# A linear-attention, GLU and MLP kernel: the first MLP pair by whole products, and a rotated decoding of GLU weights

## The chip, the cores and the metric

The kernel runs on one core of one Trainium2 chip. The metric is the device time of one execution in microseconds (us), here the median of 3 runs.

## What is computed

Three stages, all float32 in and out, cut from the reference; the weights come in as float64:

```python
q_p, k_p = phi(q * scale), phi(k * scale)         # 4 batches, 8 heads, 576 tokens, 128 random features
kv = einsum('bhsm,bhsd->bhmd', k_p, v); z = sum(k_p, axis=2)
x = (q_p @ kv) / (q_p @ z + 1e-06)                # heads side by side: 2304 tokens x 512
xn = x / sqrt(mean(x * x) + 1e-06) * rms_g
x = (silu(xn @ w_gate) * (xn @ w_val)) @ w_out    # GLU, 512 -> 1536 -> 512
out = silu(x @ w_in) @ w_out2                     # MLP, 512 -> 2048 -> 512
```

## The kernel before

**Numbers.** Every operand of a product is kept as a high and a low float32 part, and a product is three matmuls (`PASS`, line 191: high x high, high x low, low x high). A high part is made by ScalarE, the low one by VectorE as the difference (for example `split_h`, lines 196 to 200).

**Tiles.** The 2304 tokens are blocks 0 to 3 of 512 and block 4 of 256 columns. The 12 chunks of 128 columns of the GLU's inner side go three in the sweeps at the start (`sweeps`) and nine in groups u0 to u8 of one chunk each; the MLP's 16 chunks are eight pairs u9 to u16. The tiles `xs` hold the input of a stage (high and low), `ya` the sums of its output, `tok` the token sums. PSUM has four banks of tag `g` and four of tag `y`, used in turn; a product takes the next bank of its tag and waits until that has been read.

**One group.** `quad` (line 514) makes the two products of blocks 0 and 1 (gate and value, or the pair's two chunks) as seven half products, in the manner of Winograd, which need sums of the two weights (`sum12`, `sum34`) and of the tokens of blocks 0 and 1 (`tok[1]` to `tok[4]`, line 311 on). `glu_block` (line 601) and `g1_mlp` (line 233) make the other blocks by whole products. Between these pieces come the output products of earlier blocks (`g2_glu`, `g2_mlp`), a chunk at a time; VectorE adds each chunk to `ya` (line 271). In the last GLU group each chunk, once complete, is split into `xs` for the MLP by ScalarE (line 273) and VectorE (line 250).

**Token sums.** `first_sums` (line 340) makes those of the GLU from high plus low, all adds on GpSimd; `token_sums` (line 367) makes those of the MLP from `ya` in place, on GpSimd, during the last GLU group. ScalarE splits off the high half (line 329), VectorE the low one (line 332).

**Weights.** `w_load` (line 130) has SP fetch 512 KB of float64 into `raw0` or `raw1`; `w_decode` (line 141) turns them into float32 by five operations on VectorE (lines 146 to 157) and two integer adds on GpSimd (line 160). ScalarE scales a gate's or a value's weight by rms_g (line 168) and makes the high half (line 434), VectorE the low half (line 438).

**Order.** The program's order on each engine is the order in which Python emits it. `stream` (line 625) yields after each piece with the time that it costs TensorE. The driver (line 1448 on) adds that up and, in between, pops one part of the token sums after more than `T_PACE` = 1.2 us, or one job of `WeightQueue` (line 390) after more than `M_PACE` = 2.0, unless `hold` is set; `need` takes jobs early where a product wants them. The jobs of a group are the list in `plan` (line 467). Each engine works through its own instructions in that order.

Of the kernel before, what the change touches and what calls it, by code (L numbers as in the profile page):

```python
# [20 lines left out]
def kernel(  # L21
# [221 lines left out]
    def g2_glu(fs, j, hs, first, last):  # L243
# [3 lines left out]
        keep = KC // 2 if j == 1 else 0  # L247
# [7 lines left out]
        for d in range(KC):  # L255
# [57 lines left out]
    tok, sums, ready = {}, [], set()  # L313

    def w_tile(side, slot):
        pool = pools["w"][2] if side and slot < W_EARLY else pools["w"][side]
        return pool.tile([P, 2 * KC * P], F32R, tag=f"w{side}_{slot}", name=f"w{side}_{slot}")
# [22 lines left out]
    def first_sums():  # L340
# [3 lines left out]
        def temp(k, pool, tag):  # L344
            tl = pool.tile([P, KH * TB * P], F32, tag=tag, name=tag, **({"bufs": 1} if pool is rawp else {}))
            u[k] = tl.rearrange("p (c t) -> p c t", c=KH)

        def whole(k, j, h, pool, tag):
            temp(k, pool, tag)
            less(u[k], half(j, 0, h), half(j, 1, h), ALU.add)  # L350

        return [
            lambda: whole(1, 1, 0, rawp, "raw0"),
            lambda: whole(0, 0, 0, rawp, "raw1"),
            lambda: less(u[0], u[1], u[0]),
            lambda: whole(2, 1, 1, pools["w"][1], "w1_7"),
# [5 lines left out]
            lambda: whole(3, 0, 1, rawp, "raw0"),  # L362
# [1124 lines left out]
```

## Time and profile before

| | |
|---|---|
| Median of 3 runs | 976.98 us (974.52 to 978.86) |
| Profiled execution | 977.74 us |
| Its span | 975.9 us |
| Busy: TensorE, VectorE, ScalarE, GpSimd | 949.0, 712.4, 437.2, 429.6 us |
| Granted clock, mean over the span | 0.99 |

The profile is of one execution. The span runs from its first to its last instruction; the execution's own time includes what lies around it. Shares of busy time are means over stages with different limits, so the stretches are looked at one by one below. In the rows PE is TensorE (PEld its weight loads), DVE is VectorE, ACT ScalarE, POOL GpSimd, SP SyncE, and SPq its DMA queue. A row of a timeline has the start in us, the time that the x instructions of the row take together, the engine, the line, the operation, output<-input, and in brackets how long the engine was idle ahead of it and what released it. PEclk is TensorE's granted clock as a share of full speed.

### The profile page before, as it was taken

What the parts mean: (1) busy time and instruction counts of PE and PEld (TensorE: products, weight loads), DVE (VectorE), ACT (ScalarE), POOL (GpSimd) and SP (SyncE); (2) the same over time, 40 slices, a digit from 0 to 9 for tenths busy, and PEclk for the clock granted to TensorE, in tenths of its full rate; (3) what the DMA queues carried; (4) which work ended last, traced back from release to release, by engine and by line L of the source; (5) the groups of instructions that cost most, each with busy time, mean ns of one, the idle gap of its engine ahead of it and who ended that gap; (6) DMA issues with size and microseconds to landing.
All of it is one profiled execution on the core that took longest, in us unless ns stands there. A gap on an engine that the chain in (4) does not pass through costs nothing.

```text
span 975.9 us, 17017 instructions
## 1 busy us (share of the span) xinstructions
PE 949.0 (97%) x6558; PEld 793.0 (81%) x6558; DVE 712.4 (73%) x1366; ACT 437.2 (45%) x986; POOL 429.6 (44%) x414
## 2 busy tenths in 40 slices
PE   8999999999999999999999969999999999999998
PEld 6888878888787888888888847888888888888887
DVE  6998989667677698788778887547575767676643
ACT  6999886533323324433332344644243333333321
POOL 8888745625336354435445252424333332424200
PEclk9999999999999999999999979999999999999999
DMA  7655543012101121021112000202021111111023
GB/s 192 166 134 132 142 125 98 1 44 58 51 22 60 49 65 33 33 65 43 44 44 65 22 22 22 65 20 68 22 65 27 60 41 46 44 44 44 1 75 119
DMA packets 79488, 60.40 MB, mean 62 GB/s; under 512 B 27312, under 2 KB 73648, under 8 KB 79408
## 3 DMA queue, kind: packets, MB, share of 16 engines
q1 hardware_dynamic: 79136, 59.26, 21.0%
q8 instruction: 51, 0.84, 0.4%
q14 instruction: 29, 0.24, 0.1%
q10 hardware_dynamic: 272, 0.07, 0.0%
HBM read 49.87 MB, written 4.72 MB: 56 GB/s over the span
## 4 chain that ended last, share of the span: by engine, by line
PE 83%; DVE 9%; ACT 2%; POOL 2%; issue 2%; DMA 1%; SPq 1%; DVEq 0%; POOLq 0%; ACTq 0%
PE y L295 20%; PE g L205 17%; PE g L508 16%; PE y L260 10%; PE y L205 5%; PE b L957 3%; PE b L205 3%; POOL m L160 2%; PE kv L1037 2%; PE b L1357 2%; PE b L930 2%; PE b L1141 2%; DVE ya L271 1%; DVE xs L250 1%; PE b L1237 1%
## 5 line engine op out<-in xcount | busy, mean ns | idle before, releaser
L160 POOL TENSOR_TENSOR m<-m,raw 128x512 int32<-128x512 int32 x136 | 202.6, 1493 | 337.6 <-issue 179.9
L205 PE MATMUL g<-xs,w 128*128 128x512 f32 x960 | 233.1, 390 | 0.0
L205 PEld LDWEIGHTS g<-xs,w 128*128 128x128 f32 x960 | 180.0, 188 | 37.0
L295 PE MATMUL y<-w,h 128*128 128x512 f32 (+1 forms) x870 | 206.9, 388 | 0.0
L295 PEld LDWEIGHTS y<-w,h 128*128 128x128 f32 x870 | 162.5, 188 | 33.6
L260 PE MATMUL y<-h,w 128*128 128x512 f32 (+1 forms) x648 | 159.2, 373 | 12.1 <-ACT s L614 4.9
L199 DVE TENSOR_TENSOR h<-s,h 128x512 fp32r<-128x512 f32 (+1 forms) x134 | 103.0, 773 | 68.0 <-ACT h L198 66.5
L260 PEld LDWEIGHTS y<-h,w 128*128 128x128 f32 x648 | 115.1, 192 | 35.8 <-ACT s L614 5.3
L271 DVE TENSOR_TENSOR ya<-y,ya 128x512 f32<-128x512 f32 (+1 forms) x200 | 122.6, 630 | 23.3 <-PE y L260 22.9
L198 ACT ACTIVATE h<-s 128x512 fp32r<-128x512 f32 (+1 forms) x134 | 77.1, 585 | 114.1 <-DVE s L611 68.6
L306 DVE TENSOR_TENSOR ya<-y,ya 128x512 f32<-128x512 f32 (+1 forms) x127 | 84.3, 679 | 56.9 <-PE y L295 56.3
L508 PE MATMUL g<-xs,w 128*128 128x512 f32 x408 | 105.2, 393 | 0.0
L438 DVE TENSOR_TENSOR w<-m,w 128x512 fp32r<-128x512 f32 x67 | 65.9, 984 | 39.3 <-ACT w L434 39.3
L434 ACT ACTIVATE w<-m 128x512 fp32r<-128x512 f32 x76 | 47.9, 630 | 99.6 <-POOL m L160 89.6
L508 PEld LDWEIGHTS g<-xs,w 128*128 128x128 f32 x408 | 76.8, 190 | 16.0
L508 PE MATMUL g<-w,w 128*128 128x512 f32 x306 | 78.8, 393 | 3.2 <-DVE s L536 2.2
L1006 ACT ACTIVATE e<-b,nb 128x128 f32<-128x128 f32 x272 | 76.1, 425 | 7.2 <-issue 4.0
L508 PEld LDWEIGHTS g<-w,w 128*128 128x128 f32 x306 | 56.7, 188 | 15.9 <-DVE s L536 2.4
L205 PEld LDWEIGHTS y<-xs,w 128*128 128x128 f32 x480 | 61.4, 191 | 6.2 <-DVE ya L271 3.9
L205 PE MATMUL y<-xs,w 128*128 128x256 f32 x480 | 62.5, 283 | 3.1 <-DVE ya L271 3.1
L974 DVE TENSOR_REDUCE small<-b 128x4 f32<-128x512 f32 (+1 forms) x80 | 51.3, 642 | 7.1 <-PE b L957 3.6
L531 ACT ACTIVATE s<-s 128x512 f32<-128x512 f32 x25 | 15.8, 632 | 81.9 <-DVE s L536 81.9
(122 smaller groups left out, 1186.2 us busy)
## 6 DMA issues: line engine op xcount, KB each, us to landing
raw<-in_moe_w_out_dram SPq DMA_DIRECT2D x28, 512.0 KB, 3.6
raw<-in_moe_w_in_dram SPq DMA_DIRECT2D x16, 512.0 KB, 3.7
raw<-in_moe_w_gate_dram SPq DMA_DIRECT2D x12, 512.0 KB, 3.6
raw<-in_moe_w_val_dram SPq DMA_DIRECT2D x12, 512.0 KB, 3.6
qT<-e SPq DMA_DIRECT2D x72, 64.0 KB, 2.5
x<-in_k_dram SPq DMA_DIRECT2D x16, 256.0 KB, 3.8
x<-in_q_dram SPq DMA_DIRECT2D x16, 256.0 KB, 3.3
va<-in_v_dram SPq DMA_DIRECT2D x32, 128.0 KB, 4.1
```

The lines of the kernel that those rows point to most:

```text
L160: tt(out=mi, in0=mi, in1=(low if step == 5 else high).bitcast(I32), op=ALU.add)
L198: nc.scalar.activation(out=ht[:, 0, :], in_=s, func=AF.Copy)
L199: nc.vector.tensor_tensor(out=ht[:, 1, :], in0=s, in1=ht[:, 0, :].bitcast(F32), op=ALU.subtract)
L205: nc.tensor.matmul(out=ps, lhsT=w[:, a, cc * P:(cc + 1) * P], rhs=xs[j][:, c, cc, :], start=(n == 0), stop=(n == 3 * KC - 1),)
L260: nc.tensor.matmul(out=ps, lhsT=wt[1, "o", f][:, a, d * P:(d + 1) * P], rhs=hs[f][:, c, :], start=(n == 0), stop=(n == nn - 1),)
L271: nc.vector.tensor_tensor(out=y[:, d, :], in0=ps, in1=y[:, d, :], op=ALU.add)
L295: nc.tensor.matmul(out=ps, lhsT=hs[f][:, a, t * P:(t + 1) * P], rhs=wt[2, "p", f][:, c, d0:d1], start=(n == 0), stop=(n == nn - 1),)
L306: nc.vector.tensor_tensor(out=o[:, t, d0:d1], in0=ps, in1=o[:, t, d0:d1], op=ALU.add)
L438: eng.tensor_tensor(out=v[:, 1, :], in0=x, in1=v[:, 0, :].bitcast(F32), op=ALU.subtract)
L508: nc.tensor.matmul(out=ps, lhsT=w[:, a, (c0 + c) * P:(c0 + c + 1) * P], rhs=x(b, c), start=(start and n == 0), stop=(n == 3 * KH - 1), ski ...
L974: nc.vector.tensor_reduce(out=st.mx.rearrange("p (j e) -> p e j", e=2)[:, e], in_=st.ps[e], axis=AX.X, op=ALU.max)
L1006: nc.scalar.activation(out=st.e[r][:, :, h, :] if blocks4 else st.e[r][:, h, :], in_=src.rearrange("p (a f) -> p a f", a=4) if blocks4 els ...
```

## The change

1. The first MLP pair (`std`) has no `quad`: blocks 0 and 1 are done by whole products, with the last output chunks of the GLU's blocks 2, 3 and 4 ahead of each.
2. The last GLU group does its output chunks one per piece like the other groups, and splits all of block 1 into high and low like the other blocks.
3. The token sums of the MLP are made during that pair, from high plus low of `xs`, by one function for both stages; its four adds of high and low (`whole`) go to VectorE, the four differences stay on GpSimd.
4. The first value weight (u0) is loaded, and the weight queue released, in the last part of the first token sums.
5. The jobs of a GLU group are rotated: value before gate, and the high and low half of the output weight of the group before stand between the two decodes.

The core of the diff (left out: arguments for types, and the job list of the later MLP pairs, which is the old one with its loads at other jobs):

```diff
         nn = 3 * len(fs)
-        keep = KC // 2 if j == 1 else 0
...
-            if last and d >= keep:
+            if last:
                 nc.scalar.activation(out=xs[j][:, 0, d, :], in_=y[:, d, :], func=AF.Copy)
-                if d > keep:
+                if d:
                     low(d - 1)
-                if d == KC - 1:
-                    low(d)
-            if last and j == 1 and d == KC - 1:
-                sums.extend(token_sums())
             yield nn * blocks[j] / 2365
+        if last:
+            low(KC - 1)
...
+    std = next(u for u, g in enumerate(groups) if g[0] == 2)
...
-    def first_sums():
+    def token_sums(temp, end):
         half = lambda j, a, h: xs[j][:, a, KH * h:KH * (h + 1), :].bitcast(F32)
         u = {}
...
-        def whole(k, j, h, pool, tag):
-            temp(k, pool, tag)
-            less(u[k], half(j, 0, h), half(j, 1, h), ALU.add)
-
...
+        def whole(k, j, h):
+            u[k] = u[1] if k == 3 else temp(k).rearrange("p (c t) -> p c t", c=KH)
+            nc.vector.tensor_tensor(out=u[k], in0=half(j, 0, h), in1=half(j, 1, h), op=ALU.add)
+
+        ready.clear()
         return [
-            lambda: whole(1, 1, 0, rawp, "raw0"),
-            lambda: whole(0, 0, 0, rawp, "raw1"),
+            lambda: whole(1, 1, 0),
+            lambda: whole(0, 0, 0),
             lambda: less(u[0], u[1], u[0]),
-            lambda: whole(2, 1, 1, pools["w"][1], "w1_7"),
+            lambda: whole(2, 1, 1),
             lambda: less(u[1], u[2], u[1]),
             lambda: less(u[2], u[2], u[0]),
             lambda: tok_high(3, u[1]),
             lambda: (tok_low(3, u[1]), tok_high(2, u[2])),
             lambda: tok_low(2, u[2]),
-            lambda: whole(3, 0, 1, rawp, "raw0"),
+            lambda: whole(3, 0, 1),
             lambda: less(u[3], u[3], u[2]),
             lambda: None,
             lambda: tok_high(4, u[3]),
-            lambda: tok_low(4, u[3]),
-            lambda: wq.load(0, 0, 0),
+            lambda: (tok_low(4, u[3]), end(0)),
         ], [
             lambda: tok_high(1, u[0]),
-            lambda: tok_low(1, u[0]),
-            lambda: wq.load(0, 1, 1),
-        ]
-
-    def token_sums():
-        y0, y1 = (ya[j].rearrange("p (c t) -> p c t", c=KC) for j in (0, 1))
-        a0, b0, a1, b1 = y0[:, :KH], y0[:, KH:], y1[:, :KH], y1[:, KH:]
-        ready.clear()
-        return [
-            lambda: less(a1, a1, a0),
-            lambda: less(b1, b1, a1),
-            lambda: (tok_high(1, a1), less(a0, b1, a0)),
-            lambda: (tok_low(1, a1), tok_high(2, b1), less(b0, b0, b1)),
-            lambda: tok_low(2, b1),
-            lambda: tok_high(3, a0),
-            lambda: tok_low(3, a0),
-            lambda: tok_high(4, b0),
-            lambda: tok_low(4, b0),
+            lambda: (tok_low(1, u[0]), end(1)),
...
-            for slots, *fns in [
-                (0, lambda: dec(a0, 0)),
-                (0, lambda: dec(a1, 1), lambda: self.load(u, bs[0], 0)),
-                (1, lambda: hi(a0), lambda: two and self.load(u, bs[1], 1)),
-                (1, lambda: lo(a0), lambda: hi(a1)),
-                (0, lambda: lo(a1), sum12),
-                (0, sum34),
-                (1, lambda: shi(0)),
-                (0, lambda: slo(0)),
-                (1, lambda: shi(1), lambda: dec(bs[0], 0), lambda: two or self.load(u + 1, 1, 1)),
-                (0, lambda: slo(1), lambda: self.load(u + 1, 0, 0)),
-            ]:
-                self.jobs.append((slots, fns))
-            if two:
...
+            load = self.load
+            if kind == 1:
+                jobs = [
+                    (0, lambda: dec(a1, 1), lambda: load(u + 1, 1, 1)),
+                    *self.tail,
+                    (0, lambda: dec(a0, 0), lambda: load(u, bs[0], 0)),
+                    (1, lambda: hi(a1)),
+                    (0, lambda: lo(a1)),
+                    (1, lambda: hi(a0)),
+                    (0, lambda: lo(a0), sum12),
+                    (0, sum34),
+                    (1, lambda: shi(0)),
+                    (0, lambda: slo(0), lambda: dec(bs[0], 0), lambda: load(u + 1, 0, 0)),
+                    (1, lambda: shi(1)),
+                    (0, lambda: slo(1)),
+                ]
+                self.tail = [(1, lambda: hi(bs[0])), (0, lambda: lo(bs[0]))]
+            elif u == std:
+                jobs = [
+                    *self.tail,
+                    (0, lambda: dec(a1, 1), lambda: load(u, bs[1], 1)),
+                    (0, lambda: dec(a0, 0), lambda: load(u, bs[0], 0)),
+                    (0,),
+                    (1, lambda: hi(a1)),
+                    (1, lambda: lo(a1), lambda: hi(a0)),
+                    (0, lambda: lo(a0), lambda: dec(bs[0], 0), lambda: load(u + 1, 0, 0)),
+                    (0, lambda: dec(bs[1], 1), lambda: load(u + 1, 1, 1)),
+                    (0,),
+                    (1, lambda: hi(bs[0])),
+                    (1, lambda: lo(bs[0]), lambda: hi(bs[1])),
+                    (0, lambda: lo(bs[1])),
                 ]
             else:
...
+        def end(n):
+            wq.load(0, n, n)
+            wq.hold = n == 0
...
             if n == 2:
                 sums.extend(later)
-                wq.hold = False
                 wq.free += [(0, k) for k in range(6)]
...
-            done = kind == 1 and groups[u + 1][0] == 2
+            done = u + 1 == std
             hs = {j: {} for j in range(NB)}
-            yield from quad(u, iter(pend), hs)
-            if u:
+            if u == std:
+                out_of = lambda j: g2_mlp(fs, j, hs[j], True, False, False)
+                ys = iter(pend)
+                now, later = token_sums(
+                    lambda k: w_tile(1, 7, F32) if k == 2 else wq.slot(("t", k), F32),
+                    lambda n: wq.release(("t", 1 - n)),
+                )
+                yield from g1_mlp(fs[0], 0, hs[0], (), take(ys, 4))
+                yield from g1_mlp(fs[1], 0, hs[0], (), take(ys, 4))
+                sums.extend(now)
+                yield from g1_mlp(fs[0], 1, hs[1], (), ys)
+                wq.release(*wq.keys(u - 1)[1])
+                yield from g1_mlp(fs[1], 1, hs[1], (), out_of(0))
+                sums.extend(later)
+                yield from g1_mlp(fs[0], 2, hs[2], (), out_of(1))
+                yield from g1_mlp(fs[1], 2, hs[2], (), ())
+            else:
+                yield from quad(u, iter(pend), hs)
...
                 ys = chain_of(out_of(0), out_of(1))
-                k = 2 if done else 1
-                yield from glu_block(f, 2, hs[2], ys, {"g": 0, "v": k})
-                yield from glu_block(f, 3, hs[3], ys, {"g": k, "v": 2 - k})
+                yield from glu_block(f, 2, hs[2], ys, {"g": 0, "v": 1})
+                yield from glu_block(f, 3, hs[3], ys, {"g": 1, "v": 1})
                 yield from glu_block(f, 4, hs[4], ys, {"g": 1, "v": 1})
                 yield from ys
                 pend = chain_of(out_of(2), out_of(3), out_of(4))
-                if done:
-                    yield from out_of(2)
-                    pend = chain_of(out_of(3), out_of(4))
...
         for c in stream():
             due += c
-            if sums:
-                if due > T_PACE:
-                    sums.pop(0)()
+            if sums and due > T_PACE:
+                sums.pop(0)()
+                if wq.hold:
                     due = 0.0
-            elif due > M_PACE and not wq.hold and wq.tick():
+            if due > M_PACE and not wq.hold and (wq.tick() or sums):
                 due = min(due - M_PACE, M_PACE)
 
 
```

**How it moves instructions.** Two places, both on VectorE, with what each instruction waits for in brackets (DMAHW is a transfer). Lines 199, 228, 146 to 157 are the same in both kernels; line 270 is the old 271, 249 the old 250, 415 the old 438, 616 the old 611.

The start of u0, where the first two weights are decoded (m_3981 is the gate's before, m_4006 the value's). Before:

```order
L146 TENSOR_SCALAR m_3981<-raw_3922 128x512 [waits DMAHW3_49]
L149 TENSOR_SCALAR raw_3922<-raw_3922 128x512
L152 TENSOR_SCALAR m_3981<-m_3981 128x512 [waits DVE_49]
L154 TENSOR_SCALAR raw_3922<-raw_3922 128x512
L157 TENSOR_SCALAR m_3981<-m_3981 128x512 [waits DVE_49]
L228 TENSOR_TENSOR s<-s,g 128x512 [waits PE_49,Activation_49]
L199 TENSOR_TENSOR h<-s,h 128x512 [waits Activation_49]
L146 TENSOR_SCALAR m_4006<-raw_3978 128x512 [waits DMAHW4_49]
L149 TENSOR_SCALAR raw_3978<-raw_3978 128x512
```

Now (m_3979 is the value's, m_3990 the gate's):

```order
L146 TENSOR_SCALAR m_3979<-raw_3967 128x512 [waits DMAHW4_49]
L149 TENSOR_SCALAR raw_3967<-raw_3967 128x512 [waits DVE_49]
L152 TENSOR_SCALAR m_3979<-m_3979 128x512 [waits DVE_49]
L154 TENSOR_SCALAR raw_3967<-raw_3967 128x512
L157 TENSOR_SCALAR m_3979<-m_3979 128x512 [waits DVE_49]
L146 TENSOR_SCALAR m_3990<-raw_3905 128x512 [waits DMAHW3_49]
L149 TENSOR_SCALAR raw_3905<-raw_3905 128x512
L152 TENSOR_SCALAR m_3990<-m_3990 128x512 [waits DVE_49]
L154 TENSOR_SCALAR raw_3905<-raw_3905 128x512
L157 TENSOR_SCALAR m_3990<-m_3990 128x512 [waits DVE_49]
L228 TENSOR_TENSOR s<-s,g 128x512 [waits PE_49,Activation_49]
L199 TENSOR_TENSOR h<-s,h 128x512 [waits Activation_49]
```

The value's weight is decoded first, and the product and split of lines 228 and 199, which stood between the two decodes, stand behind both.

The last GLU group, output chunks of block 0 (ya_95). Before:

```order
L271 TENSOR_TENSOR ya_95<-y,ya_95 128x512 [waits PE_49] x2
L250 TENSOR_TENSOR xs_90<-ya_95,xs_90 128x512 [waits Activation_49]
L438 TENSOR_TENSOR w_1_6900<-m_6676,w_1_6900 128x512
L611 TENSOR_TENSOR s<-s,g 128x512 [waits PE_49]
L271 TENSOR_TENSOR ya_95<-y,ya_95 128x512 [waits PE_49]
L250 TENSOR_TENSOR xs_90<-ya_95,xs_90 128x512 [waits Activation_49]
L271 TENSOR_TENSOR ya_95<-y,ya_95 128x512 [waits PE_49]
L250 TENSOR_TENSOR xs_90<-ya_95,xs_90 128x512 [waits Activation_49] x2
```

Now:

```order
L270 TENSOR_TENSOR ya_95<-y,ya_95 128x512 [waits PE_49]
L249 TENSOR_TENSOR xs_90<-ya_95,xs_90 128x512 [waits Activation_49]
L199 TENSOR_TENSOR h<-s,h 128x512 [waits DVE_49,Activation_49]
L415 TENSOR_TENSOR w_2_6900<-m_6860,w_2_6900 128x512 [waits Pool_49]
L146 TENSOR_SCALAR m_6921<-raw_6868 128x512 [waits DMAHW1_49,DVE_49]
L149 TENSOR_SCALAR raw_6868<-raw_6868 128x512
L152 TENSOR_SCALAR m_6921<-m_6921 128x512 [waits DVE_49]
L154 TENSOR_SCALAR raw_6868<-raw_6868 128x512
L157 TENSOR_SCALAR m_6921<-m_6921 128x512 [waits DVE_49]
L270 TENSOR_TENSOR ya_95<-y,ya_95 128x512 [waits PE_49]
L249 TENSOR_TENSOR xs_90<-ya_95,xs_90 128x512
L146 TENSOR_SCALAR m_6944<-raw_6857 128x512 [waits DMAHW0_49]
```

The decodes of the first pair's two output weights (m_6921 and m_6944, of which the first step is shown) stand between the adds of block 0's chunks, where none stood before.

## Rows read from the trace of the kernel before

**Rows 1.** Stretches: from:to, length; busy time and instructions by engine; PEclk; DMA.

```profile
186.00:214.00 28.00, 28.00 (x159) 24.59 (x158) 13.72 (x15) 12.21 (x21) 11.33 (x5) 1.00 0.06 19
238.04:530.76 292.72, 286.38 (x1381) 240.06 (x1381) 226.30 (x400) 101.24 (x210) 133.85 (x111) 0.99 0.15 47
349.21:384.84 35.63, 35.63 (x175) 30.16 (x175) 29.84 (x56) 13.07 (x28) 16.57 (x14) 1.00 0.20 60
530.76:629.97 99.21, 87.67 (x397) 72.29 (x397) 77.87 (x121) 44.85 (x79) 37.50 (x26) 0.91 0.13 38
629.97:677.71 47.74, 47.74 (x224) 39.98 (x223) 28.93 (x51) 19.89 (x35) 16.85 (x12) 1.00 0.12 35
```

**Rows 2.** Timeline of PE in a steady group: start, duration, engine, line, operation, count.

```profile
355.86 1.52 PE L508 MATMUL g<-xs,w 128*128 128x512 f32 x6
357.22 1.52 PE L260 MATMUL y<-h,w 128*128 128x512 f32 x6
```

**Rows 3.** Timelines of VectorE, GpSimd, ScalarE and PE at u0's stall; [idle before <-releaser].

```profile
257.28 1.53 DVE L149 TENSOR_SCALAR raw<-raw 128x512 uint32<-128x512 uint32 x1
257.16 2.80 POOL L160 TENSOR_TENSOR m<-m,raw 128x512 int32<-128x512 int32 x2 [3.92 <-issue]
264.08 1.28 ACT L168 ACTIVATE m<-m,g_sb 128x128 f32<-128x128 f32 x4 [2.13 <-POOL m L160]
265.92 0.61 ACT L198 ACTIVATE h<-s 128x512 fp32r<-128x512 f32 x1
268.12 1.87 DVE L271 TENSOR_TENSOR ya<-y,ya 128x512 f32<-128x512 f32 x3
268.85 2.35 PE L205 MATMUL y<-xs,w 128*128 128x256 f32 x12 [2.12 <-DVE ya L271]
```

**Rows 4.** Timelines of GpSimd, VectorE and PE in the transition to the MLP.

```profile
571.44 5.97 POOL L320 TENSOR_TENSOR ya<-ya,ya 128x1024 f32<-128x1024 f32 x2
571.83 3.38 DVE L332 TENSOR_TENSOR xs<-ya,xs 128x1024 fp32r<-128x1024 f32 x1
572.77 1.65 PE L260 MATMUL y<-h,w 128*128 128x512 f32 x3 [4.86 <-ACT s L614]
578.88 1.65 PE L260 MATMUL y<-h,w 128*128 128x512 f32 x3 [4.45 <-DVE s L611]
583.88 1.55 PE L508 MATMUL g<-xs,w 128*128 128x512 f32 x6
```

**Rows 5.** Timelines of VectorE and GpSimd: the same operations alone and beside GpSimd.

```profile
213.95 1.22 DVE L332 TENSOR_TENSOR xs<-raw,xs 128x1024 fp32r<-128x1024 f32 x1
550.32 0.68 DVE L438 TENSOR_TENSOR w<-ws,w 128x512 fp32r<-128x512 f32 x1
552.81 3.03 POOL L160 TENSOR_TENSOR m<-m,raw 128x512 int32<-128x512 int32 x2 [4.22 <-issue]
554.60 1.79 DVE L438 TENSOR_TENSOR w<-m,w 128x512 fp32r<-128x512 f32 x1
358.52 2.47 DVE L271 TENSOR_TENSOR ya<-y,ya 128x512 f32<-128x512 f32 x4
```

**Rows 6.** Start of u0: timelines of SP, VectorE and PE, and DMA issues there.

```profile
215.20 0.37 SPq L136 DMA_DIRECT2D raw<-in_moe_w_val_dram  x1
raw<-in_moe_w_val_dram SPq DMA_DIRECT2D x1, 512.0 KB, 3.4
216.29 0.41 DVE L146 TENSOR_SCALAR m<-raw 128x512 uint32<-128x512 uint32 x1
217.96 0.68 DVE L228 TENSOR_TENSOR s<-s,g 128x512 f32<-128x512 f32 x1
219.34 0.69 DVE L199 TENSOR_TENSOR h<-s,h 128x512 fp32r<-128x512 f32 x1 [0.70 <-ACT h L198]
219.94 2.93 PE L260 MATMUL y<-h,w 128*128 128x512 f32 x12
229.23 2.10 PE L260 MATMUL y<-h,w 128*128 128x512 f32 x8 [0.56 <-DVE h L199]
```

More of the change, by code (lines that the diff above doesn't have):

```diff
@@ L391, in __init__ @@
         def __init__(self):
-            self.jobs, self.st, self.hold, self.free, self.held = [], {}, True, [], {}
+            self.jobs, self.st, self.hold, self.free, self.held, self.tail = [], {}, True, [], {}, []
             for u in range(len(groups)):
@@ L419, in plan @@
         def plan(self, u):
+            kind, _ = groups[u]
             (a0, a1), bs = self.keys(u)
@@ L423, in plan @@
             ss.t = {}
-            two = len(bs) == 2
             hw = KH * P
@@ L463, in slo @@
             def slo(n):
-                split_lo(ss.x if n == 0 else mf(a1), ss.t[n], nc.vector if two else nc.gpsimd)
+                split_lo(ss.x if n == 0 else mf(a1), ss.t[n], nc.vector if kind == 2 else nc.gpsimd)
                 wt["s", u, n] = ss.t[n]
-            for slots, *fns in [
-                (0, lambda: dec(a0, 0)),
-                (0, lambda: dec(a1, 1), lambda: self.load(u, bs[0], 0)),
-                (1, lambda: hi(a0), lambda: two and self.load(u, bs[1], 1)),
-                (1, lambda: lo(a0), lambda: hi(a1)),
-                (0, lambda: lo(a1), sum12),
-                (0, sum34),
-                (1, lambda: shi(0)),
-                (0, lambda: slo(0)),
-                (1, lambda: shi(1), lambda: dec(bs[0], 0), lambda: two or self.load(u + 1, 1, 1)),
-                (0, lambda: slo(1), lambda: self.load(u + 1, 0, 0)),
-            ]:
-                self.jobs.append((slots, fns))
@@ L480, in plan @@
-            if two:
-                self.jobs += [
-                    (1, [lambda: hi(bs[0]), lambda: dec(bs[1], 1)]),
-                    (0, [lambda: lo(bs[0]), lambda: self.load(u + 1, 1, 1)]),
-                    (1, [lambda: hi(bs[1])]),
-                    (0, [lambda: lo(bs[1])]),
-                ]
-            else:
-                self.jobs += [(1, [lambda: hi(bs[0])]), (0, [lambda: lo(bs[0])])]
+            load = self.load
[29 more added lines that the diff above has]
+                    (0, lambda: lo(bs[1])),
+                ]
+            else:
+                jobs = [
+                    (0, lambda: dec(a0, 0)),
+                    (0, lambda: dec(a1, 1), lambda: load(u, bs[0], 0)),
+                    (1, lambda: hi(a0), lambda: load(u, bs[1], 1)),
+                    (1, lambda: lo(a0), lambda: hi(a1)),
+                    (0, lambda: lo(a1), sum12),
+                    (0, sum34),
+                    (1, lambda: shi(0)),
+                    (0, lambda: slo(0)),
+                    (1, lambda: shi(1), lambda: dec(bs[0], 0)),
+                    (0, lambda: slo(1), lambda: load(u + 1, 0, 0)),
+                    (1, lambda: hi(bs[0]), lambda: dec(bs[1], 1)),
+                    (0, lambda: lo(bs[0]), lambda: load(u + 1, 1, 1)),
+                    (1, lambda: hi(bs[1])),
+                    (0, lambda: lo(bs[1])),
+                ]
@@ L490, in tick @@
+            self.jobs += [(n, fns) for n, *fns in jobs]
         def tick(self):
@@ L619, in glu_block, with take @@
         hs[f] = split_h(s, j)
+    def take(ys, n):
+        for _ in range(n):
+            c = next(ys, None)
+            if c is not None:
+                yield c
     def chain_of(*its):
@@ L628, in stream, with temp @@
         order = [(3, f0), (4, f0), (1, [f2]), (0, [f2]), (2, [f2]), (3, [f2]), (4, [f2])]
-        now, later = first_sums()
+        def temp(k):
+            if k == 2:
+                return w_tile(1, 7, F32)
+            return rawp.tile([P, KH * TB * P], F32, tag=f"raw{1 - k % 2}", name=f"raw{1 - k % 2}", bufs=1)
+        def end(n):
+            wq.load(0, n, n)
+            wq.hold = n == 0
+        now, later = token_sums(temp, end)
         sums.extend(now)
@@ L667, in stream @@
                 out_of = lambda j, end=False: g2_mlp(fs, j, hs[j], first, last, end)
-                for n, f in enumerate(fs):
-                    yield from g1_mlp(f, 2, hs[2], (), out_of(1 - n))
+                if u != std:
+                    for n, f in enumerate(fs):
+                        yield from g1_mlp(f, 2, hs[2], (), out_of(1 - n))
                 if last:
```

14 lines of the change are left out of this document (7 added, 7 removed).

## The prediction

> **What bounds the kernel now.** I read the busy summary first (TensorE 97% of the span), so time can only come from the few stretches in which TensorE waits, from its low clock, or from matmuls. The view of busy time by stretch then tells which stretches those are [rows 1]. A clean GLU group takes 35.63 us with TensorE busy throughout; a clean MLP group takes 47.74 us, again without idle time. The eight groups u0 to u7 take 292.72 us. Six 512-column matmuls start 1.36 us after one another's first, 0.2267 us each [rows 2]. u0 has 12 of these fewer than the groups after it, so the eight would take 8 x 35.63 - 2.72 = 282.3 us clean: **10.4 us are lost there**. The last GLU group has 12 more (38.35) and the first MLP pair 36 more (43.79), 82.1 us clean, and they take 99.21 at a mean granted clock of 0.91: **17.1 us are lost there**. What follows is bound by TensorE and is not changed.
>
> *Why the groups lose* is read in the timelines around u0's stall [rows 3]. Two weight decodes come back to back. In the second one two steps on VectorE take 1.53 us each in place of 0.42, beside GpSimd's two adds for the first (2.80). The result reaches ScalarE late: its scale waits 2.13 us at 264.08, the split of h (line 198) is queued behind it, VectorE adds the three chunks at line 271 from 268.12 on, and TensorE's next matmul waits 2.12 us for a bank. Its 12 matmuls then take 2.35 us. *Why the transition loses* is in [rows 4]: TensorE stands still for 4.86 and 4.45 us, and the 12 matmuls that begin at 578.88 (3, 6 and 3) take until 583.88, 5.00 us against 12 x 0.2267 = 2.72, so a gap of that kind costs 2.3 us more at the low clock. At that time two token-sum splits on VectorE take 3.38 us each or nearly, beside two sums on GpSimd that take 5.97.
>
> **The price of sharing.** A low half on VectorE takes 0.68 us alone and 1.79 us where GpSimd's adds run; the 128 x 1024 form takes 1.22 alone and 3.38 beside a sum. An add that reads PSUM keeps its 0.6 us per chunk beside GpSimd (4 in 2.47) [rows 4, 5]. So what this change puts on VectorE from SBUF is priced once clean and once with a wait. The Trainium skill (SBUF — State Buffer, section Who interferes with whom) says the same in a stronger form: such a VectorE instruction and a GpSimd instruction that reads SBUF exclude each other, and the later one is blocked for the whole of the other. By that alone every new add and decode of the transition could wait, and the sum would be the high end given below, +11.7; by the clean rows it would be the low end, -6.6. The trace agrees with the page in the rows just named, but shows that many such operations find GpSimd idle.
>
> **The change, part by part.**
>
> *Rotation of the GLU jobs.* A group's two decodes no longer follow each other: the two halves of the previous group's output weight lie between them, so GpSimd has some two paces more to finish the first, and VectorE does not queue behind its adds. No instruction is added; the same load is issued on SP, up to a decode earlier. Following a steady group through the new order with the durations above, VectorE's adds free each bank at least 2 us before TensorE wants it. I take the whole loss as gone, **-10.4**; the least is -8, since two small idles of u6 and u7 may stay.
>
> *Start of u0 (a new wait).* Before, u0's gate weight was decoded first; its bytes had long been in. Now its value weight is first. That transfer is issued at 215.20, when its buffer comes free, and lands 3.4 us later, at 218.6 [rows 6]. VectorE reaches the decode at about 216.3, where the gate's decode began before, and stands at it. The first excerpt of the order shows what is queued behind it: this decode, then the other decode, and only then the product at line 228 and the low half of h on which TensorE's matmuls at 219.94 wait. Clean, five steps take 217.96 - 216.29 = 1.67 us; the second decode runs beside the first one's adds on GpSimd and takes 1.67 + 2 x (1.53 - 0.42) = 3.9 [rows 3, 6]. So line 228 starts at 218.6 + 1.7 + 3.9 = 224.2 in place of 217.96, and TensorE 1.98 us later as before, at 226.2 in place of 219.94: 6.2 us of idle. The idle 0.56 at 229.23 goes. A gap of this length brings the low clock, +2.3. Sum **+7.9**; 5.5 if the second decode finds GpSimd free, 8.5 if line 199 waits for it too.
>
> *First sums (lines 340 to 365 before).* Four 128 x 1024 adds go from GpSimd to VectorE, 4 x 1.22 = 4.9 us there. From 186 to 214 TensorE is busy for all of 28.00 us and VectorE for 13.72 [rows 1], so I cost them at nothing; the cover is TensorE's products, and without it they would cost the 4.9.
>
> *First pair by whole products.* Seven half products of 6 matmuls become four wholes of 12: 6 matmuls x 0.2267 = **+1.36**. The pair's two weight sums and their splits fall away, and TensorE needs no token sum before the next pair.
>
> *Work of VectorE in the transition.* Counted in the order between the start of the last GLU group and the end of the first pair, it gets two decodes more (8 for 6: 3.3 clean, 7.8 beside GpSimd), four 128 x 1024 adds of high and low that the sums didn't need before, being made of ya (4.9 by the 1.22 of the split of that size), two low halves of block 1 more and one of weights fewer (+0.7), and two combinations of 0.68 fewer: +7.5 clean, +12 with waits, where it is busy 77.87 of 99.21 us already [rows 1]. The second excerpt of the order shows the place: behind the last GLU quad there are two decodes, and the two of the output weights come between the adds of block 0's chunks, so that each add that must free a bank has a decode ahead of it. Following the order there with the prices of [rows 5, 6]: TensorE, clean, arrives at block 4's value product 17.1 us after the quad; that takes the bank of block 1's first output chunk, which VectorE would have added by 17.4 clean, and by 24.4 with GpSimd's adds in the way. 7.4 us are lost there, in three waits (3.25, 2.33, 1.86). The backlog doesn't shrink: the last add of block 3 ends at 51.4 where TensorE would be at 33.8, a loss of 17.6. While the token sums are made another 7.0 come, since ScalarE's token half waits for a subtraction on GpSimd with the split of h behind it. Loss 24.5 for 17.1, on a clean time of 83.5 for 82.1: the stage takes 108.0 for 99.2, **+8.8**. Bounds: a loss of 14 (half of the adds and decodes hidden in VectorE's 21 idle us) gives -1.7; 27 (all of them with a wait) gives +11.2. Loads move too: a pair's first output weight is asked for one decode earlier on SP; each is in before its decode except the one at the start.
>
> **The sum.** -10.4 + 7.9 + 8.8 = +6.3 us. The profiled execution took 977.74 us (span 975.9), 0.8 above the median of 976.98, so its time becomes 984.0 and the median **983.3 us**. The ends: -10.4 + 5.5 - 1.7 = -6.6, and -8 + 8.5 + 11.2 = +11.7. About 0.5% (4.9 us) is what a measurement of this kernel can tell from no change.
>
> **Rivals.**
> - *The transition works as a pipeline (faster).* The gap at 572.77 and 578.88 is caused by TensorE's quad asking for token sums; whole products ask for none. If VectorE's queue keeps up within two banks' time of the adds, some 3 us of the 17.1 stay: stage 86.5, -12.7. With start and groups as above -15.2: **962**. It decides at block 1's first output chunk: its add must end within 17.1 us of the quad. For it: VectorE is idle 21 us of the stage. Against: those idles are waits in a chain, and the new work stands ahead of the adds. Chance 0.18.
> - *The backlog is as long as before, no longer.* Stage between -3 and +2, total -5.5 to -0.5: **974**. 0.18 (0.06 of it faster by over 0.5%).
> - *No wait at the start,* as the transfer or the adds are out of the way by then: -10.4 + 8.8 = -1.6, **975**. 0.06.
> - *The rotation removes no stall in u0 to u7:* the decodes still meet GpSimd, now with a low half of the output weight in the same queue, and the losses stay: +16.7, **993**. 0.08.
>
> **How the numbers follow.** My forecast has 0.50, with a range of its own of 974 to 989; 0.38 of it lies above 981.9 (slower by over 0.5%) and 0.12 between. Faster: 0.18 + 0.06 = 0.24. Same: 0.12 + 0.12 + 0.06 = 0.30. Slower: 0.38 + 0.08 = 0.46. The range of 963 to 991 takes in the four cases but the lower half of the first rival and the tails of the last and of mine.
>
> **What would show it.** The span of the eight groups: about 282 us from the first to the last GLU quad, and no idle of over 0.5 us ended by line 270 (the old 271). At the start: an idle of about 6 us of TensorE before the matmuls that follow the first group's h, ended by line 199, with line 146 on VectorE waiting for a transfer. In the transition: TensorE's idles ended by line 270 rather than by the token sums, a stage of 100 to 110 us, VectorE busy over 85 us. Wrong it is if TensorE passes the transition with under 10 us of idle time, or if the first decode of u0 starts without a wait.

## The result and the profile after

| | before | changed |
|---|---|---|
| Median | 976.58 us (4 runs) | 986.07 us (984.44 to 987.23, 4 runs) |
| Ratio to before | | 1.0095 (95% interval 1.0067 to 1.0124) |
| Profiled execution: span | 975.9 us | 982.7 us |

The change makes the kernel slower by 9.5 us by the medians, 6.8 by the two spans. The profiled execution of the changed kernel (984.44 us) is the fastest of its four; the other three had a lower mean granted clock (0.984 to 0.986 for 0.991), and no trace shows where their further time lies. Measured from the first matmul of one quad to that of another, the difference of the spans lies here ("transition" below means the last GLU group and the first pair, and "clean" the time with TensorE busy throughout at full clock):

| stretch | before | changed | difference | forecast |
|---|---|---|---|---|
| up to the 24 matmuls ahead of u0's wait | 214.50 | 213.27 | -1.2 | 0 |
| from there to the first quad | 23.37 | 29.65 | +6.3 | +7.9 |
| u0 to u7 | 292.73 | 282.36 | -10.4 | -10.4 |
| last GLU group and first pair | 99.37 | 110.78 | +11.4 | +8.8 |
| seven pairs behind, end | 345.93 | 346.64 | +0.7 | 0 |

(The windows of [rows 1] begin 0.16 us behind the first matmuls that this table counts from, hence 99.21 there and 99.37 here.) The first row's -1.2 is no effect of the change: in ten kernels of the experiments that are the same up to there, the 24 matmuls begin between 213.04 and 215.84. The second row moves too: two of those kernels (e_late, e_noadd) have the changed start as a whole, and took 31.13 and 31.18 us for it, 7.8 more than the kernel before.

Stretches of the changed kernel, columns as in [rows 1]:

```profile
242.92:525.28 282.36, 282.36 (x1381) 239.05 (x1380) 204.21 (x388) 98.19 (x208) 125.42 (x104) 1.00 0.15 45
525.28:636.06 110.78, 91.88 (x404) 74.01 (x403) 83.39 (x131) 44.50 (x78) 39.84 (x27) 0.94 0.12 39
```

The eight groups now keep TensorE busy for the whole stretch, 282.36 of 282.36 us. The transition takes 110.78 us, with TensorE busy for 91.88 of it and a granted clock of 0.94; before, these were 99.21, 87.67 and 0.91 [rows 1]. So its idle time rose from 11.5 to 18.9 us, and its busy time by 4.2, of which six more matmuls are 1.4.

The start of u0, timelines of VectorE and TensorE (compare [rows 6]):

```profile
217.32 0.43 DVE L146 TENSOR_SCALAR m<-raw 128x512 uint32<-128x512 uint32 x1 [2.19 <-DMA raw<-in_moe_w_val_dram]
219.34 1.50 DVE L149 TENSOR_SCALAR raw<-raw 128x512 uint32<-128x512 uint32 x1
222.86 0.68 DVE L228 TENSOR_TENSOR s<-s,g 128x512 f32<-128x512 f32 x1
213.27 5.60 PE L205 MATMUL g<-xs,w 128*128 128x512 f32 x24
224.25 4.65 PE L259 MATMUL y<-h,w 128*128 128x512 f32 x12 [5.38 <-ACT h L198]
```

VectorE stands 2.19 us at the value's decode, waiting for its transfer. The second decode goes from 219.01 to 222.86, with steps of 1.50 us beside GpSimd's adds. Only then come line 228 and h, and TensorE idles 5.38 us; its next 12 matmuls take 4.65 us where they took 2.93, at a mean granted clock of 0.66.

The transition, timelines of VectorE and of TensorE's longest waits (compare [rows 4]):

```profile
560.65 1.50 DVE L146 TENSOR_SCALAR m<-raw 128x512 uint32<-128x512 uint32 x1
564.02 3.09 DVE L249 TENSOR_TENSOR xs<-ya,xs 128x512 fp32r<-128x512 f32 x2
559.40 1.63 PE L205 MATMUL y<-xs,w 128*128 128x256 f32 x12 [2.54 <-DVE ya L270]
564.15 0.97 PE L259 MATMUL y<-h,w 128*128 128x512 f32 x3 [3.12 <-DVE ya L270]
567.77 2.93 PE L205 MATMUL y<-xs,w 128*128 128x256 f32 x12 [2.65 <-DVE ya L270]
582.69 0.96 PE L259 MATMUL y<-h,w 128*128 128x512 f32 x3 [1.69 <-DVE ya L270]
595.49 4.51 PE L205 MATMUL g<-xs,w 128*128 128x512 f32 x12
613.13 6.66 PE L292 MATMUL y<-w,h 128*128 128x512 f32 x21 [2.79 <-ACT h L198]
```

TensorE waits for line 270, the add that frees a bank, and at the end for h (line 198); eleven waits add up to 18.9 us. The decode's step at 560.65 (1.50 us in place of 0.42) and the low halves at 564.02 (3.09 us for two) run beside GpSimd's integer adds (558.88 to 561.87 and 563.58 to 566.57), and stand ahead of the next add. The 12 matmuls at 595.49 take 4.51 us, at a mean granted clock of 0.62, behind waits of 0.76 and 1.18 us.

### The profile page after: what moved, and what is told of

The parts are those of the page before. It is cut to its first block, busy times and chain, and to the rows that moved or that the text cites. A ratio compares the mean times of both kernels' runs of the same rounds, so it can differ in the third digit from the quotient of the medians.

```text
span 982.7 us, 17038 instructions
## 1 busy us (share of the span) xinstructions
PE 949.7 (97%) x6564; PEld 794.2 (81%) x6564; DVE 699.1 (71%) x1372; ACT 433.6 (44%) x983; POOL 416.5 (42%) x406
## 4 chain that ended last, share of the span: by engine, by line
PE 86%; DVE 7%; ACT 2%; DMA 2%; POOL 2%; issue 1%; SPq 1%; DVEq 0%; POOLq 0%
PE g L205 20%; PE y L292 20%; PE g L513 16%; PE y L259 12%; PE y L205 5%; PE b L992 3%; PE b L205 2%; PE b L1392 2%; PE kv L1072 2%; PE b L1176 2%; PE b L965 1%; DVE xs L249 1%; DVE ya L270 1%; POOL m L160 1%; PE b L1152 1%
## 5 line engine op out<-in xcount | busy, mean ns | idle before, releaser
L160 POOL TENSOR_TENSOR m<-m,raw 128x512 int32<-128x512 int32 x136 | 204.9, 1509 | 341.2 <-issue 193.5
L205 PE MATMUL g<-xs,w 128*128 128x512 f32 x1008 | 245.9, 391 | 0.0
L205 PEld LDWEIGHTS g<-xs,w 128*128 128x128 f32 x1008 | 189.9, 189 | 39.4
L292 PE MATMUL y<-w,h 128*128 128x512 f32 (+1 forms) x870 | 209.1, 390 | 3.9 <-ACT h L198 2.8
L259 PEld LDWEIGHTS y<-h,w 128*128 128x128 f32 x648 | 114.2, 190 | 38.4 <-DVE ya L270 10.4
L513 PE MATMUL g<-xs,w 128*128 128x512 f32 x384 | 97.8, 390 | 0.0
L411 ACT ACTIVATE w<-m 128x512 fp32r<-128x512 f32 x75 | 47.1, 628 | 86.5 <-POOL m L160 73.9
L513 PEld LDWEIGHTS g<-xs,w 128*128 128x128 f32 x384 | 71.5, 188 | 14.8
L415 DVE TENSOR_TENSOR w<-m,w 128x512 fp32r<-128x512 f32 x66 | 59.6, 902 | 22.6 <-ACT w L411 22.6
L513 PE MATMUL g<-w,w 128*128 128x512 f32 x288 | 73.3, 390 | 0.0
L513 PEld LDWEIGHTS g<-w,w 128*128 128x128 f32 x288 | 53.5, 188 | 10.7
L536 ACT ACTIVATE s<-s 128x512 f32<-128x512 f32 x23 | 14.5, 632 | 80.1 <-DVE s L541 80.1
```

The costliest lines, as they stand in the source:

```text
L160: tt(out=mi, in0=mi, in1=(low if step == 5 else high).bitcast(I32), op=ALU.add)
L205: nc.tensor.matmul(out=ps, lhsT=w[:, a, cc * P:(cc + 1) * P], rhs=xs[j][:, c, cc, :], start=(n == 0), stop=(n == 3 * KC - 1),)
L259: nc.tensor.matmul(out=ps, lhsT=wt[1, "o", f][:, a, d * P:(d + 1) * P], rhs=hs[f][:, c, :], start=(n == 0), stop=(n == nn - 1),)
L292: nc.tensor.matmul(out=ps, lhsT=hs[f][:, a, t * P:(t + 1) * P], rhs=wt[2, "p", f][:, c, d0:d1], start=(n == 0), stop=(n == nn - 1),)
L415: eng.tensor_tensor(out=v[:, 1, :], in0=x, in1=v[:, 0, :].bitcast(F32), op=ALU.subtract)
L513: nc.tensor.matmul(out=ps, lhsT=w[:, a, (c0 + c) * P:(c0 + c + 1) * P], rhs=x(b, c), start=(start and n == 0), stop=(n == 3 * KH - 1), ski ...
```

## The experiments

Twelve kernels ran. Their edits are shown shortened, a list by the names of its jobs: dec is a weight's decode, hi and lo its two halves, shi and slo those of a weight sum, a0 and a1 the first two weights of a group (gate and value, or the pair's two), b its output weights, tail the two halves left from the group before, and (0,) an empty job. Behind each time stand the ratio to the kernel before and its 95% interval. The lengths of stretches are of one trace each. My theory was: at the start two decodes ahead of u0's h; in the transition VectorE's queue, with decodes and waits for GpSimd ahead of the adds. The rivals: at the start the transfer alone; in the transition the sum of VectorE's and GpSimd's work, which no other order would shorten.

### The start: e_gate and e_gap

```diff
# e_gate: in u0 the jobs' order
-dec(a1) + load, *tail, dec(a0) + load
+dec(a0) + load, *tail, dec(a1) + load
# e_gap: the same with an empty job between
+dec(a0) + load, (0,), dec(a1) + load
```

> The changed kernel with one edit: in u0 the gate's weight is decoded before the value's (its transfer is in early), both still ahead of line 228. My theory (two decodes ahead of the product, of which the late transfer is only a part): the first decode runs at 214.5 without a wait, the second waits for the transfer until 217.3 and runs beside GpSimd's adds for 3.9 us, so line 228 starts at about 221.2 in place of 222.86 and TensorE's idle falls from 5.4 to about 3.7 us: 1.7 us less, about 984. Rival (the late transfer is all of it): the idle goes, 6 to 7 us less, about 979.

Measured: 984.57 us (1.0085, 1.0062 to 1.0108). The wait for the transfer shrinks to 0.79 us, line 228 starts at 220.61, TensorE idles 3.35 us, and from its 24 matmuls to the first quad it takes 28.12 us for 29.65: 1.5 less, no more than the 1.5 by which traces of the changed start differ (29.65 to 31.18), so the waits have to decide. Counted from the start of the 24 matmuls, line 228 starts 9.6 us later in the changed kernel, 7.6 here and 3.5 in the kernel before. Of the 6.1 us lost in the changed kernel 2.2 are the wait for the transfer and 3.9 the second decode; here it is 0.8 and 3.2. So the late transfer was the smaller part, and the rival, that it is all, is out.

> The same, with the gate's decode first and one empty job between the two decodes, so that lines 228 and 199 stand between them as in the kernel before. My theory: the idle of 5.4 us and the 1.7 us of low clock behind it go, 6 to 7 us less than the changed kernel, about 979, and the groups u0 to u7 keep their 282.4 us. Rival (the second decode stalls u0 later, as it did in the kernel before, where 2.1 us of idle and a low clock stood at 268.85): 3 us less at most.

Measured: 979.36 us (1.0025, 1.0013 to 1.0036), 6.7 less than the changed kernel, which is the number I gave. The reason is only in part the one I gave. The wait of 5.38 is gone, but the second decode now makes the next h late. TensorE's timeline of e_gap:

```profile
219.61 2.94 PE L259 MATMUL y<-h,w 128*128 128x512 f32 x12
229.66 0.49 PE L259 MATMUL y<-h,w 128*128 128x512 f32 x1 [1.67 <-ACT h L198]
230.69 4.01 PE L259 MATMUL y<-h,w 128*128 128x512 f32 x11 [0.54 <-DVE h L199]
```

The same eleven matmuls in e_apart (below), whose start is the same:

```profile
231.05 2.79 PE L259 MATMUL y<-h,w 128*128 128x512 f32 x11 [0.54 <-DVE h L199]
```

From the 24 matmuls at 214.17 to the first quad e_gap takes 26.80 us, 2.85 less than the changed kernel. That looks like the rival's "3 us at most", but one trace of each does not settle it: behind the same two waits the eleven matmuls take 4.01 us here, at a mean granted clock of 0.66, and 2.79 in e_apart, at 1.00. Seven kernels with this start take 25.16 to 26.80 us, three with the changed one 29.65 to 31.18, so the start is worth 2.9 to 6.0 us. In these two traces another 3.7 us came in the transition (107.11 us for 110.78), whose code is the same: one empty job at u0 moved its jobs against TensorE's pieces, eight groups later. In e_gate, where the order of the transition is that of the changed kernel, it took 111.1.

### The rotation alone: e_rot

```diff
 # in the kernel before
-jobs of a GLU group: dec(a0), dec(a1), hi(a0), ... hi(b), lo(b)
+dec(a1), hi and lo of the b before, dec(a0), hi(a1), ... (gate first in u0)
```

> The kernel before with the rotated list of GLU jobs alone (gate first in u0, nothing else of the change: first pair by quad, token sums made of ya in the last GLU group). My theory: the rotation alone is worth the 10.4 us, u0 to u7 take about 282.4 us, the transition stays near 99.2 us (up to 104, since its jobs now start two later), about 966 to 971. Rival (the groups gained from the other parts): u0 to u7 stay at about 292 us, 976.

Measured: 989.31 us (1.0126, 1.0110 to 1.0143). Neither expectation held. Stretch of u0 to u7, and TensorE's timeline in one group and in the first pair:

```profile
238.25:527.24 288.99, 284.76 (x1382) 238.43 (x1381) 231.93 (x388) 100.54 (x208) 129.86 (x104) 1.00 0.15 44
403.12 0.50 PE L260 MATMUL y<-h,w 128*128 128x512 f32 x1 [0.51 <-DVE w L439]
606.04 0.50 PE L295 MATMUL y<-w,h 128*128 128x512 f32 x1 [3.88 <-ACT w L435]
```

The stalls of [rows 3] are gone, but every group from u1 on now takes 36.43 us or a little more and has a wait of 0.51 for the low half of an output weight: 289.0 us for the eight. The granted clock stays at 1.00; of the 0.80 us that a group loses, the 0.29 beyond the wait lie in the matmuls next to it. The list is the one of the changed kernel; there the same half is done 19.9 us behind the quad's start, here 21.6. What differs is where the queue starts to run and how the driver paces it, which no run varied alone. So the gain of 10.4 needs more than the rotated list. The transition took 113.9 us, 14.5 more than before, with the old pair and the old sums, and with waits for late weights (3.88 in the row shown).

### The kind of product: e_quad and e_q0

```diff
 # in e_gap: the transition of the kernel before
-if u == std: g1_mlp(...) whole products, token_sums(temp, end)
+quad(u, iter(pend), hs), token sums of ya on GpSimd in the last GLU group
```

> The kernel of the run e_gap (changed, start mended) with the transition of the kernel before: first pair by quad, token sums made of ya on GpSimd during the last GLU group, its old job list behind the two halves left from the last GLU group. My theory (the gain is the rotation's, once its queue has its lead; the loss is the new transition's): u0 to u7 stay near 282.4 us and the transition returns to 99 to 104 us, so 967 to 972, below both kernels. Rival (the groups' gain hangs on the new pair or its sums): u0 to u7 go back to 290 us, 976 or more, as in the run e_rot.

Measured: 982.86 us (1.0080, 1.0055 to 1.0105). Neither expectation held: the groups keep 282.4 us, but the transition of the kernel before, behind the rotated queue, takes 112.0 us and not 99.4. Stretch, and timelines of VectorE and TensorE:

```profile
523.21:635.23 112.02, 91.90 (x398) 74.22 (x397) 85.52 (x131) 46.80 (x81) 47.48 (x32) 0.89 0.13 38
563.05 2.60 DVE L146 TENSOR_SCALAR m<-raw 128x512 uint32<-128x512 uint32 x1
565.57 2.56 DVE L149 TENSOR_SCALAR raw<-raw 128x512 uint32<-128x512 uint32 x1
571.66 1.65 PE L260 MATMUL y<-h,w 128*128 128x512 f32 x3 [7.00 <-ACT s L629]
```

The decode of the pair's output weight meets the token sums on GpSimd: two of its steps take 2.60 and 2.56 us. Behind it in VectorE's queue stands the product of line 626, behind that on ScalarE the split of h and line 629, and for that TensorE waits 7.00 us. So the new products and sums are not needed for a transition of this length: behind the rotated queue the old ones take as long (and in e_rot, too). What the new ones would cost behind the old list, this does not show.

```diff
 # e_q0, in e_quad
-shi(1) + dec(b0), slo(1) + load, hi(b0) + dec(b1)
+shi(1), slo(1), dec(b0), load, hi(b0) + dec(b1)
```

> The kernel of e_quad with one edit: the decodes of the first pair's output weights some jobs later, behind the two token splits that TensorE's quad waits for (in e_quad the first of them stood ahead, with two steps of 2.60 and 2.56 us beside GpSimd's sums, and TensorE waited 7.00 us). My theory (position of a decode, not the kind of product, sets the transition): that wait falls to 2 to 4 us, the later one for the output weights (3.77) grows by 1 to 3: 978 to 981 in place of 982.9. Rival (the rotated queue is late as a whole in the transition): no change within 1.5 us.

Measured: 980.92 us (1.0035, 1.0024 to 1.0047). The wait of 7.00 falls to 3.66, that for the output weights grows from 3.77 to 4.88, as forecast: moving one decode past two splits moves waits of this size. But TensorE's idle time in the transition is 20.1 us in both, and the stretch takes 110.5 us for 112.0: the waits changed places more than they shrank. (The edit stands in the list of all pairs; the pair behind the first stays at 47.75 us.)

### GpSimd and the decodes: e_noadd, e_pool, e_late

```diff
 # e_noadd, in the changed kernel
-for k in range(7): w_decode(...)
+for k in range(5 if u == std else 7): w_decode(..., down=u == std)
 # e_pool
-nc.vector.tensor_tensor(out=u[k], in0=half(j, 0, h), in1=half(j, 1, h), op=ALU.add)
+less(u[k], half(j, 0, h), half(j, 1, h), ALU.add)
 # e_late
-lo(a0) + dec(b0) + load, dec(b1) + load, (0,), hi(b0), ...
+lo(a0), six (0,), dec(b0) + load, two (0,), dec(b1) + load, (0,), hi(b0), ...
```

> The changed kernel, with the two integer adds on GpSimd left out for the four weights of the first pair (and that pair's shift on VectorE turned round so that the values stay finite; the first pair's products are then of other numbers). VectorE does the same instructions. My theory (decodes, low halves and sums on VectorE wait for GpSimd's adds): VectorE's waits on them go, some 7 us by its rows, and ScalarE's on the adds: the transition of 110.8 us falls by 8 to 14 us, about 972 to 978. Rival (VectorE's own work and order set it): at most 3 us less, 983 or more.

Measured: 977.01 us (1.0013, 0.9998 to 1.0027); in the transition, columns as above:

```profile
529.03:630.98 101.95, 90.35 (x403) 72.18 (x402) 79.37 (x131) 44.63 (x78) 27.04 (x19) 0.95 0.14 42
```

101.95 us for 110.78: 8.8 less, and 9.1 less by the medians. Waiting for the integer adds of four weights, directly and through ScalarE, is worth about a third of the 27.3 us that the changed transition loses.

> The changed kernel with the four adds of high and low of both token sums on GpSimd again, as in the kernel before (at the start and in the first pair). My theory: VectorE loses 4.9 us of work in the transition, GpSimd gets 9.6 us, which block VectorE's low halves in the same place: within 3 us of 986. Rival (the adds on VectorE are a cause of the new loss): 4 us less or more, 982 or below.

Measured: 985.97 us (1.0104, 1.0080 to 1.0128), transition 111.2 us. (less() runs on GpSimd.) On which of the two engines the four adds of high and low run makes no difference; what they would be worth if left out was not tried.

> The changed kernel with the decodes of the first pair's two output weights seven and ten jobs later, behind the adds of blocks 0 and 1. My theory (VectorE's decodes ahead of the adds that free banks make the waits of 2.54, 3.12 and 2.65 us at block 4's products, 8.3 us with a low clock behind them): these three go; what comes back depends on the backlog, the adds of blocks 2 and 3 now have the two decodes ahead, so 3 to 8 us less, about 978 to 983. Rival (VectorE's sum of work sets the stage, whatever its order): within 2 us of 986. Rival (the output weights come too late): longer, with TensorE waiting at line 292.

Measured: 984.11 us (1.0074, 1.0057 to 1.0091), transition 108.4. The three waits at block 4 fall from 8.3 to 1.1 us, and the output weights come late; TensorE's timeline of e_late:

```profile
597.63 8.01 PE L292 MATMUL y<-w,h 128*128 128x512 f32 x23 [6.36 <-DVE w L415]
```

So the decodes' place does make those waits, and moving them alone exchanges them for one of 6.36 us.

### Toward a faster version: e_mid, e_mid5, e_apart, e_apart2

```diff
 # e_mid, in e_gap
-lo(a0) + dec(b0) + load, dec(b1) + load, (0,), hi(b0), ... lo(b1)
+lo(a0), three (0,), dec(b0) + load, (0,), dec(b1) + load, (0,), hi(b0), ... lo(b1), three (0,)
 # e_mid5, in e_mid: pace of the sums' parts from the first pair on
-if sums and due > T_PACE
+if sums and wait > 2.4
 # e_apart, in e_mid (e_apart2: 1.6 for 1.8)
+if sums and wait > 1.8, the rest over carried on; five (0,) behind lo(b1)
```

> The kernel of e_gap with the decodes of the first pair's output weights behind the adds of block 1 and their halves ahead of the token sums, and the next pair's jobs three later. My theory: the two waits at block 4's products (2.43 and 4.38 us in e_gap) shrink below 2 us in sum, and the wait for the output weights that e_late brought (6.36 us) is gone since their halves come before the sums: 5 to 9 us less than e_gap's 979.4, so 970 to 974. Rival (VectorE's sum of work sets the stage): the idle comes back at blocks 3 and 4 and at line 292, 977 to 981.

Measured: 978.02 us (1.0017, 1.0004 to 1.0030), transition 106.3. My theory's 970 to 974 missed. The waits at block 4's value products fell to one of 0.76 us, and waits of 1.96, 1.16, 2.54 and 4.93 us stand at line 292: what the rival said.

> The kernel of e_mid with one edit: the parts of the token sums made during the first pair come every 2.4 us of TensorE's work in place of 1.2. My theory (in e_mid the two waits of 2.54 and 4.93 us at line 292 are ScalarE's and VectorE's split of h queued behind token halves that wait for GpSimd's subtractions, and the next pair's two decodes blocked by the same subtractions): those two waits fall from 7.5 to under 2.5 us in sum: 5 to 7 us less than e_mid, 971 to 973, 4 to 6 us below the kernel before. Rival (VectorE's sum of work): the idle comes back in other places or in the next pair, since the sums end later: 976 to 980.

Measured: 984.43 us (1.0073, 1.0046 to 1.0099), above both expectations. The transition took 101.5 us, 4.8 less; but the next pair took 59.64 for 47.74. TensorE's timeline there:

```profile
627.50 0.50 PE L522 MATMUL g<-xs,w 128*128 128x512 f32 x1 [1.63 <-ACT xs L327]
649.67 0.74 PE L292 MATMUL y<-w,h 128*128 128x512 f32 x2 [1.61 <-DVE w L416]
652.84 3.65 PE L292 MATMUL y<-w,h 128*128 128x512 f32 x7 [2.43 <-ACT w L412]
```

It waits for the last token sum (line 327) and then for its own output weights: the work was put off, not saved.

> The kernel of e_mid with the parts of the token sums every 1.8 us on the mean (e_mid5: at least 2.4, which made them late for the next pair) and the next pair's jobs two later, so that the split of h stands ahead of that pair's two decodes and a token split between them. My theory (position of each decode against an h, an add or a subtraction): the transition falls from 106.3 to 101 to 104 us and the next pair stays at 47.74: 973 to 976, at or just below the kernel before. Rival (VectorE's and GpSimd's sum of work in the transition and the pair behind it is the bound): what the transition gains the next pair loses again, 977 to 982.

> The same with the parts every 1.6 us on the mean (both decodes then stand one token split later). My theory: within 2 us of e_apart, next pair at 47.74. Rival: as for e_apart, 977 to 982.

Measured: 977.12 us (1.0004, 0.9993 to 1.0014) and 978.46 us (1.0026, 1.0013 to 1.0039), transitions 106.8 and 107.7, next pair 47.75. e_apart is level with the kernel before; no version beat it. My theory's 101 to 104 us for the transition missed, and so did the rival's account, since the transition gained nothing that the next pair could lose. The longest wait that is left stands in TensorE's timeline of e_apart:

```profile
612.49 1.22 PE L292 MATMUL y<-w,h 128*128 128x512 f32 x2 [5.14 <-ACT h L198]
```

## Why the prediction was right

The time, 986.07, lies in the range and in the forecast's own case, 2.8 above the point. The mechanism was right in the main: clean groups, a new wait at the start, a transition with more waits for the adds that free banks. That the sum of the spans (+6.8 for +6.3) comes so close is partly luck, as errors within the parts go both ways. Of the signs named, the idle of TensorE at the start was ended by line 198 and not 199, the transition took 110.8 us (100 to 110 named), and VectorE was busy 83.39 us in it (over 85 named); the others held.

- *Groups, -10.4:* -10.4 measured. The stall of [rows 3] was two decodes in a row, and without it a group is clean. What the step left out is a condition, shown by e_rot: with the start and the pace of the kernel before, the list gave 3.7.
- *Start, +7.9:* +6.3. The wait for the transfer, the second decode of 3.9 us (3.85) and the queue of line 228 behind both came as worked out. VectorE, the transfer and TensorE's 24 matmuls were all about 1.2 us earlier than in the kernel before, which changes no wait. TensorE's idle was 5.38 for 6.2 since one distance was misread: "TensorE 1.98 us later as before" takes the matmuls at 219.94 to have waited for h, but their row in [rows 6] has no idle time; where they do wait they come 1.39 us behind line 228 (224.25 for 222.86). The slower matmuls behind the wait cost 1.7 for 2.3 in this trace; the 12 matmuls took 4.65 us here, 5.79 in e_late and 5.74 in e_noadd behind much the same wait, so those two traces come out at +7.8. (With the second decode clean, the step's own numbers give 5.7, not the 5.5 of its low end.)
- *Transition, +8.8:* +11.4. The first waits were where the order showed them (2.54, 3.12 and 2.65 us for 3.25, 2.33 and 1.86). The sum was not made up as forecast: idle time 18.9 us for 24.5, and 8.4 us of slower matmuls (91.88 busy for 83.5 clean), which that term did not hold. The two errors, -5.6 and +8.4, cancel in part, by luck.
- *The step that failed* is the count that explained this term: "two decodes more ..., four 128 x 1024 adds ...". Taking the four adds off VectorE again changed nothing (e_pool), so their place in its queue is not what costs. And the term was booked as the new pair's work, where the rotated queue is enough for it: with the old pair and the old sums behind that queue the transition is as long or longer (112.0 us in e_quad, 113.9 in e_rot). GpSimd's integer adds, which were in the count as waits, are worth 8.8 us (e_noadd), and the place of the output weights' decodes makes the first three waits (e_late).
- *The rule on shared access*, that the later of the two is blocked for the whole of the other (the Trainium skill, SBUF — State Buffer, section Who interferes with whom): the runs agree where it applies. Two steps of a decode take 2.60 and 2.56 us in place of 0.42, each beside a sum on GpSimd, in e_quad.
- *Rivals.* "The transition works as a pipeline" is out, 110.8 us for its 86.5. "The backlog is as long as before" is out by +11.4, "no wait at the start" by the 5.38 us. "The rotation removes no stall" is out for the changed kernel, and nearly true of e_rot.

Left open: whole products with the list of the kernel before were not tried, so what the new pair is worth by itself is not known. Nor is it shown why e_apart's transition stays at 107 us; that VectorE's and GpSimd's sum of work bounds it is the rival that four runs (e_mid, e_mid5, e_apart, e_apart2) failed to break, not a measured bound. VectorE alone is not the bound: it is busy for 88.0 of the 106.8 us there.

## What to carry to other kernels

Where one queue hands out jobs between the pieces of another engine's work, an edit to its list changes where all later jobs stand: read the order at the next change of stage, too, not only where the stall was. Price a decode by what stands behind it in its engine's queue, and by what GpSimd runs beside it. An expected gain that arrives may still have another source: compare it stretch by stretch, as for e_gap, and with more than one trace, since the same start took 25.16 us in one kernel and 26.80 in another.

## What the runs showed of the hardware

A wait costs TensorE more than its idle time. In e_rot a wait of 0.51 us made each group 0.80 us longer, with the granted clock at 1.00 throughout. In the changed transition eleven waits, none above 3.2 us, stand beside 8.4 us by which TensorE's busy time exceeds the clean one. By the 0.29 us that a wait of e_rot cost besides, about 3 us of that would be there at full clock, too (an estimate, 11 x 0.29); the mean granted clock of 0.94 can make at most about 7 (0.06 of 110.78 is 6.6). I had counted slower matmuls only behind waits of 4 us and more, but 12 of them took 4.51 us in place of 2.72 behind waits of 0.76 and 1.18, at a granted clock of 0.62.

The same waits do not always bring the low clock (0.5, that is 1.2 GHz in place of 2.4): behind 1.67 and 0.54 us it came in e_gap (a mean of 0.66 over the next eleven matmuls) and not in e_apart (1.00). Behind 5.4 to 5.8 us at the start it came in all three traces of the changed start, but the 12 matmuls had a mean of 0.66 in the changed kernel and 0.50 in e_late. A difference of 1.5 us between two traces can be this alone.
